# Nine instead of twelve unread matmuls ahead of x of block 0, and w_v in two transfers

## The chip, the cores and the metric

The kernel runs on one core of a Trainium2 chip. The metric is the device time in microseconds of one execution; for the kernel before it is the median of four runs. The engines are named as the profile names them: PE (TensorE, matmul), PEld (its weight load), DVE (VectorE), ACT (ScalarE), POOL (GpSimd) and SP (SyncE). POOL and SP issue nearly all DMA transfers.

## The reference

Two layers follow each other, in fp32, with B = 4, N = 6208 and C = 256. The first is an attention between channels: q and k are divided by their norms over the 6208 rows, their 256 x 256 product goes through a softmax, and v is multiplied by it. The second is a channel mix on x, the first one's output: each row is blended with the row before it, once for k and once for r.

```
qn = q / (norm(q, axis=1) + 1e-6);   kn = k / (norm(k, axis=1) + 1e-6)
a  = softmax(kn.T @ qn / tau, axis=-1)          # per batch 256 x 256
x  = v @ a                                      # B x 6208 x 256
x_prev = x moved down by one row, zeros first
xk = mu_k * x + (1 - mu_k) * x_prev
xr = mu_r * x + (1 - mu_r) * x_prev
k  = max(xk @ w_k, 0)                           # w_k: 256 x 1024
out = sigmoid(xr @ w_r) * (k * k @ w_v)         # w_v: 1024 x 256, w_r: 256 x 256
```

## The kernel before

The rows of a batch go in 12 groups of 512 and one of 64. The program has a head for batch 0 and then one long loop; the instruction order of every engine is fixed by the order in which the program is written (the planner that could reorder it is off).

**The head.** SP loads q and k of batch 0 in fp32 (line 102). DVE casts each piece to bf16, ACT squares it, and PE adds the product of k and q into `s_ps` (line 152) and the squares into `nq_ps` and `nk_ps` (line 119). Once the last k piece is in, the end of the softmax runs as a chain over the engines: POOL takes the root of the norms of k (line 165), DVE their inverse (170, 172), ACT the exponential with row sums (208), DVE the inverse sums and the scaled matrix `a_sb`, in two halves of 128 rows (617, 618). Meanwhile PE transposes v of block 0 (line 258) and one small matmul turns `mu` (604). Then PE runs `filler(F1)` (line 605, the matmuls at line 198): F1 matmuls of 512 columns whose sum nobody reads. After them comes x of block 0, `x_first` (line 279): four matmuls that need both halves of `a_sb`, in the order first half for both column halves, then second half. ACT casts one column half of x to bf16 (281) and DVE the other (282).

**The loop.** A block is 512 rows of one batch; there are 48 of them and one more block for the left-over rows. The work of a block is cut in eight steps `j`, and three blocks are in hand at a time: x and the blends of block i + 2, the up-projection of block i + 1 (`up`, line 343, for block 0 partly line 338), and the gate (`gate_mm`, 364) and down-projection of block i (`down`, 403). The first step of `down` takes the feature tiles 0 to 2 of `kk` and `w_v_sb` for a quarter of the rows, the second step tiles 3 to 7, and so on:

```
for fh in (range(3) if h == 0 else range(3, 8)):
    nc.tensor.matmul(v_ps[:, s % 2], kk[:, fh, s * P:(s + 1) * P], w_v_sb[:, fh, :], ...)
```

Between these matmuls PE works on the covariance of the next batch in units (`unit`, 447), for which q and k arrive in groups (`group_load`, 436). ACT casts x and takes the rectifier of the up-projection (347), DVE squares it (354).

**POOL's queue.** The transfers that cast fp32 to bf16 are issued by POOL, in the order of the program: v of block 0, half of w_k, v of block 1, the other half of w_k, v of block 2, the 64-row group of batch 1 (`more_rows(1)`), and then, after the root of line 165, group 0 (`more_rows(2)`), w_r, w_v, v of block 3, group 1 (`more_rows(3)`), v of block 4, and in the loop the further blocks and groups. These transfers take eight semaphores in turn, so POOL issues each only once the transfer eight places ahead of it has landed; some wait besides for their buffer. The first down-projection matmul of the loop waits for w_v's semaphore; the first gate matmul waits for w_r's.

Of the kernel before, what the change touches and what calls it, by code (L numbers as in the profile page):

```python
# [18 lines left out]
def kernel(  # L19
# [13 lines left out]
    nc = tc.nc  # L33
# [3 lines left out]
    P = 128  # L37
# [37 lines left out]
    w_v_sb = const.tile([P, 8, D], BF16, name="w_v_sb")  # L75
# [15 lines left out]
    hk = {}  # L91
    NF = 8
    LEAD = 8
    F1, FQ, F3 = 12, 3, 0
    NPE = 4

    NW = 2
# [137 lines left out]
    def v_load(i):  # L235
        b, t = blocks[i]
        v_bf = pq.tile([P, S, C], BF16, name="v_bf", tag="b2", bufs=NB + 1)
        nc.gpsimd.dma_start(v_bf, v[b, t * M:(t + 1) * M, :].rearrange("(s p) c -> p s c", p=P))  # L238
        st[i, "v"] = v_bf
# [369 lines left out]
    nc.vector.tensor_scalar(omu, mu_k_t, -1.0, 1.0, op0=OP.mult, op1=OP.add)  # L609
    more_rows(2)  # L610
    nc.gpsimd.dma_start(w_r_sb, moe_w_r.rearrange("(ko ki) d -> ki ko d", ki=P))
    nc.gpsimd.dma_start(w_v_sb, moe_w_v.rearrange("(fo fi) d -> fi fo d", fi=P))
    v_load(3)
    more_rows(3)
    v_load(4)
# [23 lines left out]
    for i in range(-2, NBLK):  # L639
        for j in range(8):  # L640
# [32 lines left out]
            if n < NBLK:  # L673

                d = 4 if n != 1 else 3
# [79 lines left out]
```

## Time and profile before

| what | us |
|---|---|
| median of 4 runs | 507.19 (506.98 to 507.80) |
| the profiled execution, its own time | 507.23 |
| its span | 505.5 |
| PE busy | 490.5 (97%) |
| DVE busy | 446.2 (88%) |
| ACT busy | 429.8 (85%) |
| POOL busy | 106.5 (21%) |
| w_v, 512 KB, from issue to landing | 9.4 |
| w_r, 128 KB, from issue to landing | 7.5 |

The span is what the profiler saw from the first to the last instruction; the time of the execution is a little longer. All points of time below count from the span's start. Busy matmul time is modelled at its end,[...] so starts are more exact than ends. A few matmul records are missing from the trace. In the row of 40 slices one slice is 12.6 us and a digit is a share in tenths. In a timeline a line gives the start, the time taken by the run of equal instructions, the engine, the line, the operation and its operands, and in square brackets how long the engine had been idle and what ended that. In the view of waits a line gives who waited for whom, the total in us, how often, and the longest.

### The profile page before, as it was taken

The numbers are of one execution on the slowest core, as the hardware profiler recorded it, in microseconds if no ns is written. First come the engines' busy times: TensorE is split into PE (matmuls) and PEld (weight loads), VectorE is DVE, ScalarE is ACT, GpSimd is POOL, SyncE is SP. The second block draws the span as 40 slices with busy tenths as digits, with TensorE's granted clock in tenths as the row PEclk, the third lists the DMA queues.
The fourth block names the chain that finished last, engine by engine and source line by source line (L and its number), as shares of the span: only waits on it lengthen the run. The fifth ranks groups of instructions, "written<-read, shape, count | busy, mean of one in ns | idle before, by whom it ended". The sixth has DMA issues, their size and how long they took to land.

```text
span 505.5 us, 9692 instructions
## 1 busy us (share of the span) xinstructions
PE 490.5 (97%) x3643; PEld 339.8 (67%) x3706; DVE 446.2 (88%) x704; ACT 429.8 (85%) x806; POOL 106.5 (21%) x150
## 2 busy tenths in 40 slices
PE   5899999999999999999999999999999999999997
PEld 2575677777666766676667666667666666666675
DVE  3568898999999999999999999999999787887875
ACT  6778999999998998998998899899878777777774
POOL 0057523332521321221341132100031000000000
PEclk9999999999999999999999999999999999999999
DMA  8999999999999999899699999973259743344123
GB/s 333 384 334 190 191 202 207 204 198 192 180 179 197 192 195 157 122 169 167 108 183 216 184 173 157 155 149 85 62 113 185 152 99 96 95 78 92 41 84 105
DMA packets 143271, 83.48 MB, mean 165 GB/s; under 512 B 50740, under 2 KB 140024, under 8 KB 143224
## 3 DMA queue, kind: packets, MB, share of 16 engines
q0 software_dynamic: 66080, 33.01, 51.7%
q1 hardware_dynamic: 77000, 49.79, 42.8%
q8 instruction: 29, 0.48, 0.4%
q14 instruction: 18, 0.15, 0.1%
q10 hardware_dynamic: 144, 0.07, 0.0%
HBM read 78.71 MB, written 25.43 MB: 206 GB/s over the span
## 4 chain that ended last, share of the span: by engine, by line
PE 88%; DMA 7%; DVE 1%; issue 1%; ACT 1%; SPq 1%; POOL 1%; ACTq 0%
PE v_ps L403 33%; PE kT_ps L343 30%; PE g_ps L364 9%; PE xT_ps L269 8%; PE s_ps L447 6%; DMA f<-in_k_dram 3%; DMA f<-in_q_dram 2%; DMA w_v_sb<-in_moe_w_v_dram 2%; PE v_ps L392 1%; SPq L102 1%; PE s_ps L152 1%; POOL qk L436 0%; DVE xk L322 0%; DVE kk L354 0%; PE n_ps L502 0%
## 5 line engine op out<-in xcount | busy, mean ns | idle before, releaser
L347 ACT ACTIVATE kr<-kT_ps 128x512 bf16<-128x512 f32 (+1 forms) x392 | 232.5, 597 | 38.1 <-PE kT_ps L343 29.8
L403 PE MATMUL v_ps<-w_v_sb,kk 128*128 128x256 bf16 x1520 | 228.3, 273 | 1.0 <-DMA w_v_sb<-in_moe_w_v_dram 0.2
L343 PE MATMUL kT_ps<-xk,w_k_sb 128*128 128x512 bf16 (+1 forms) x721 | 217.1, 377 | 0.7
L403 PEld LDWEIGHTS <-kk 128*128 128x128 bf16 x1520 | 148.4, 98 | 57.8 <-DVE kk L354 0.4
L354 DVE TENSOR_TENSOR kk<-kr 128x1024 bf16<-128x1024 bf16 (+1 forms) x196 | 132.9, 679 | 30.6 <-ACT kr L347 29.7
L451 ACT ACTIVATE sq<-qk 128x512 f32<-128x512 bf16 (+1 forms) x147 | 93.4, 635 | 0.0
L343 PEld LDWEIGHTS <-w_k_sb 128*128 128x128 bf16 x780 | 75.2, 98 | 22.0 <-issue 0.9
L364 PE MATMUL g_ps<-w_r_sb,xr 128*128 128x256 bf16 x388 | 73.6, 273 | 1.6
L271 ACT CAST X<-xT_ps 128x512 bf16<-128x512 f32 x94 | 55.6, 592 | 19.4 <-PE xT_ps L269 18.7
L322 DVE SCALAR_TENSOR_TENSOR xr<-delta,mu_t,X 128x512 bf16<-128x512 bf16 x96 | 71.2, 743 | 0.0
L364 PEld LDWEIGHTS <-xr 128*128 128x128 bf16 x388 | 37.9, 98 | 44.6 <-issue 0.7
L322 DVE SCALAR_TENSOR_TENSOR xk<-delta,mu_t,X 128x512 bf16<-128x512 bf16 x96 | 67.8, 744 | 0.0
L416 DVE SCALAR_TENSOR_TENSOR res<-res,v_ps 128x512 f32<-128x512 f32 x95 | 64.4, 678 | 0.0
L436 POOL DMA_DIRECT2D qk<-in_q_dram x39 | 28.7, 735 | 159.4 <-ACT sq L451 138.3
L409 ACT ACTIVATE res<-g_ps 128x512 f32<-128x512 f32 x97 | 57.8, 598 | 0.0
L269 PE MATMUL xT_ps<-vT,a_sb 128*128 128x512 bf16 x188 | 56.1, 379 | 0.1
L447 PE MATMUL s_ps<-qk 128*128 128x256 bf16 (+1 forms) x294 | 56.1, 272 | 0.1
L485 DVE TENSOR_TENSOR acc<-acc,sq 128x1024 f32<-128x1024 f32 x44 | 53.5, 1215 | 0.1
L238 POOL DMA_DIRECT2D v_bf<-in_v_dram x48 | 37.0, 773 | 59.6 <-DMA vT<-v_bf 39.5
L447 PEld LDWEIGHTS <-qk 128*128 128x128 bf16 (+1 forms) x294 | 27.8, 98 | 12.3 <-issue 0.8
L311 DVE TENSOR_TENSOR delta<-X 128x1024 bf16<-128x1024 bf16 x48 | 32.9, 685 | 0.1
L436 POOL DMA_DIRECT2D qk<-in_k_dram x39 | 28.7, 736 | 6.5 <-DMA qk<-in_q_dram 2.1
(86 smaller groups left out, 231.6 us busy)
## 6 DMA issues: line engine op xcount, KB each, us to landing
out_dram<-res SPq DMA_DIRECT2D x47, 512.0 KB, 4.2
v_bf<-in_v_dram POOLq DMA_DIRECT2D x48, 256.0 KB, 9.1
qk<-in_q_dram POOLq DMA_DIRECT2D x36, 256.0 KB, 9.6
qk<-in_k_dram POOLq DMA_DIRECT2D x36, 256.0 KB, 10.9
f<-in_q_dram SPq DMA_DIRECT2D x12, 512.0 KB, 7.4
f<-in_k_dram SPq DMA_DIRECT2D x10, 512.0 KB, 8.8
f<-in_k_dram SPq DMA_DIRECT2D x3, 256.0 KB, 7.8
vT<-v_bf SPq DMA_TRANSPOSE x44, 7.7
```

The source lines that it names most:

```text
L269: nc.tensor.matmul(xT_ps, a_sb[:, b, ih, dh * P:(dh + 1) * P], vT[:, :, ih, :], start=ih == 0, stop=ih == 1)
L322: nc.vector.scalar_tensor_tensor(o[:, dh], st[i, "d"][:, dh], mu[:, dh:dh + 1], X[:, dh, c:c + M], op0=OP.mult, op1=OP.add)
L343: nc.tensor.matmul(kT_ps[:, :m], w_k_sb[:, dh, fh * P:(fh + 1) * P], xk[:, dh, :m], start=dh == 0, stop=dh == 1)
L347: nc.scalar.activation(st[i, "kr", fh // 2][:, fh % 2, :m], kT_ps[:, :m], AF.Relu, scale=RH)
L354: nc.vector.tensor_tensor(st[i, "kk"][:, fh - 1:fh + 1, :m], kr[:, :, :m], kr[:, :, :m], op=OP.mult)
L364: nc.tensor.matmul(g_ps[:, s % 2], xr[:, dh, s * P:(s + 1) * P], w_r_sb[:, dh, :], start=s % 2 == 0 and dh == 0, stop=dh == 1, skip_group_ ...
L403: nc.tensor.matmul(v_ps[:, s % 2], kk[:, fh, s * P:(s + 1) * P], w_v_sb[:, fh, :], start=s % 2 == 0 and fh == 0, stop=fh == 7, skip_group_ ...
L409: nc.scalar.activation(st[i, "res"][:, 2 * u:2 * u + 2], st.pop((i, "g", u)), AF.Tanh, scale=0.5)
L416: nc.vector.scalar_tensor_tensor(r, r, 1.0, st.pop((i, "v", u)), op0=OP.add, op1=OP.mult)
L436: nc.gpsimd.dma_start(qk[:rows, :n, i], src_rows(t, b, g))
L447: nc.tensor.matmul(cov[b][:, ih, :], qk[:rows, s, 1, ih * P:(ih + 1) * P], qk[:rows, s, 0, :], start=g == GORD[0] and s == 0 and ih == 0, ...
L451: nc.scalar.activation(G["sq", s // 2][:rows, s % 2], qk[:rows, s], AF.Square)
```

## The change

F1 becomes 9, so three matmuls of `filler(F1)` fall away. The load of w_v, a single transfer on POOL's queue, becomes two in the same place: feature tiles 0 to 2, and then tiles 3 to 7.

```diff
-    F1, FQ, F3 = 12, 3, 0
+    F1, FQ, F3 = 9, 3, 0
...
     nc.gpsimd.dma_start(w_r_sb, moe_w_r.rearrange("(ko ki) d -> ki ko d", ki=P))
-    nc.gpsimd.dma_start(w_v_sb, moe_w_v.rearrange("(fo fi) d -> fi fo d", fi=P))
+
+    w_v = moe_w_v.rearrange("(fo fi) d -> fi fo d", fi=P)
+    nc.gpsimd.dma_start(w_v_sb[:, :3], w_v[:, :3])
+    nc.gpsimd.dma_start(w_v_sb[:, 3:], w_v[:, 3:])
     v_load(3)
     more_rows(3)
     v_load(4)
```

In the instruction order of PE, six rows fall away (three weight loads and three matmuls); POOL has one row more; nothing else changes its place. The first down-projection matmul then waits for the first of the two transfers, and the fourth for the second. From v of block 3 on, every POOL transfer stands one place further in the turn of the eight semaphores.

## The prediction

> **What bounds the kernel now.** I read the page's head first, then the chain that ended last in order of time, then the timelines of PE, DVE, ACT and POOL between 38 and 64 us, and last the transfers' times to landing.
>
> ```profile
> span 505.5 us, 9692 instructions
> PE 490.5 (97%) x3643; PEld 339.8 (67%) x3706; DVE 446.2 (88%) x704; ACT 429.8 (85%) x806; POOL 106.5 (21%) x150
> DMA  8999999999999999899699999973259743344123
> PE f_ps L198 <- DVE qb L134: 6.5, 4, 5.3
> PE s_ps L152 <- DVE kb L147: 1.5, 4, 0.5
> PE v_ps L403 <- DMA w_v_sb<-in_moe_w_v_dram: 0.2, 1, 0.2
> ```
>
> The last three lines are all that the view of waits has for PE over the whole span. The first two belong to the load-bound head before 35 us. The third is the only later one, and it is at the transfer that the change splits. From start to start, PE's matmuls after 57 us follow each other at 0.11 us (256 columns) and 0.22 us (512), apart from holes of one matmul's size, which are lost records. So a microsecond that PE gains before 57 us should still be there at the end, provided that data keep arriving.
>
> ```profile
> 38.46 0.72 POOL nrm_r L165
> 39.18 1.51 POOL qk L436 x2
> 40.69 0.67 POOL w_r_sb L611
> 41.36 9.39 DMA w_v_sb<-in_moe_w_v_dram
> 50.75 0.04 issue
> 50.79 0.49 PE v_ps L403 x3
> ```
>
> This is the chain in order of time. Up to 50.79 us it does not run through PE: it runs through POOL's issues and w_v's transfer, and only from there on PE to the end. Removing unread matmuls alone should therefore buy nothing; w_v would still land at 50.75.
>
> ```profile
> 38.89 2.76 PE L198 MATMUL f_ps<-qb,ident 128*128 128x512 bf16 x11
> 41.49 1.03 PE L279 MATMUL x_ps<-vT,a_sb 128*128 128x512 bf16 x4
> 50.22 0.38 PE L364 MATMUL g_ps<-w_r_sb,xr 128*128 128x256 bf16 x2
> 50.79 0.49 PE L403 MATMUL v_ps<-w_v_sb,kk 128*128 128x256 bf16 x3 [0.20 <-DMA w_v_sb<-in_moe_w_v_dram]
> 52.42 0.71 PE L403 MATMUL v_ps<-w_v_sb,kk 128*128 128x256 bf16 x5
> ...
> 40.44 0.42 DVE L618 TENSOR_TENSOR a_sb<-e_sb,sm 128x256 bf16<-128x256 f32 x1
> 40.98 0.42 DVE L618 TENSOR_TENSOR a_sb<-e_sb,sm 128x256 bf16<-128x256 f32 x1
> 42.55 0.69 DVE L282 CAST X<-x_ps 128x512 bf16<-128x512 f32 x1 [0.75 <-PE x_ps L279]
> ```
>
> Here are the two places of the change. The twelve unread matmuls (eleven recorded, twelve weight loads) end exactly where x of block 0 starts, at 41.49; but x's second factor, a_sb, was complete at 40.98 + 0.42 = 41.40. PE, not the softmax, sets x's start, by little. Later the first three down-projection matmuls wait for w_v; the other five feature tiles are wanted only at 52.42.
>
> **Part 1, nine unread matmuls.** One costs (41.49 - 38.89)/12 = 0.217 us. Three fewer: PE is free at 41.49 - 0.65 = 40.84. x's four matmuls go: both column halves with a_sb's first half, then both with its second. The first half is written at 40.44 + 0.42 = 40.86; in this trace a cast of k ended at 29.09 and its matmuls began at 29.15, so I add 0.06: the first pair starts at 40.92 and has issued by 41.35. The second half is there at 41.40, so the third starts at 41.46, not at 41.49 + 2 x 0.217 = 41.92. **Gain 0.46 of the 0.65 removed**; the rest turns into waits for DVE (0.08 and 0.11).
>
> Does the stage behind follow? ACT casts x's first half at 42.33 and DVE the second at 42.55; 0.46 earlier both are still free (ACT's last scaling of w_k ends at 41.50, DVE's at 41.80). From there ACT and DVE work nearly without a pause up to 50 us and pace PE, but everything hangs on x. Transfers don't move, so each must land before its new need: v of block 1 33.88 + 6.8 = 40.7 (needed 41.9), w_k's second half 34.84 + 7.1 = 41.9 (needed about 46.2), v of block 2 44.3 (47.7), the 64-row k group 44.8 (48.2), the first full k group 39.93 + 7.5 = 47.4 (49.0), w_r 40.67 + 7.5 = 48.2 (49.8). None binds, so PE reaches the first down-projection 0.46 earlier.
>
> [...]
>
> **Part 2, w_v in two transfers.** PE's g_ps pair starts at 50.22 and takes 2 x 0.109, so v_ps could have started at 50.44; it started at 50.79. The stall is 0.35 (the view's 0.20 counts from the modelled end). With part 1 alone it becomes 0.81. Now the first three tiles: the queue delivers in order, w_r has landed at 48.2, and w_v's 512 KB take until 50.75, 2.55 us. Three eighths are 0.96: **landing 49.2**, needed at 50.44 - 0.46 = 49.98. The stall is gone, with 0.8 us to spare. The other five eighths land at 50.75 plus what one transfer more costs; they are needed at 52.42 - 0.81 = 51.6. Spare: 0.85 us.
>
> What does one transfer more cost in the queue? Bounds: nothing, if bytes alone count[...]. The rows: w_r's 128 KB land 0.8 after the transfer ahead of them, and 512 KB at 2.55 would give 0.64 for that size; the two 32 KB pieces of the small group land 0.2 apart, against 0.16. So 0.05 to 0.15 in a full queue; I take 0.1, nearest to w_r, and 50.85 is still in time. [...]I take the rows: the DMA share is 9 tenths in every slice of the first third[...].
>
> POOL issues one instruction more, about 0.75 us like its neighbours. The larger effect is its eight semaphores in turn: each transfer waits for the one eight places before, and now one later.
>
> ```profile
> 41.36 0.94 POOL L612 DMA_DIRECT2D w_v_sb<-in_moe_w_v_dram  x1
> 42.49 0.76 POOL L238 DMA_DIRECT2D v_bf<-in_v_dram  x1 [0.19 <-PE x_ps L279]
> 44.66 0.74 POOL L436 DMA_DIRECT2D qk<-in_q_dram  x1 [1.41 <-DMA v_bf<-in_v_dram]
> 51.03 0.74 POOL L436 DMA_DIRECT2D qk<-in_k_dram  x1 [1.63 <-DMA w_v_sb<-in_moe_w_v_dram]
> ```
>
> w_v's second part waits for w_k's second half (landed 41.9), so it goes out at about 42.2. v of block 3 now waits for v of block 2, which put it at 44.66 (its old successor's place): **2.2 us later than 42.49**. Behind it q and k of group 1 slip to about 45.4 and 46.1, v of blocks 4 to 6 to 46.9, 47.6 and 48.4 (or 0.3 behind w_r's landing, which is POOL's step from 50.75 to 51.03; the same), q of group 2 waits for w_v's first part (49.5 against 48.65), and k of group 2 for the second (51.03, plus the 0.1). From then on each waits for the same predecessor as before. Is the queue empty meanwhile? At 45.4 it still holds q and k of group 0, w_r and w_v, with data up to 50.75, so v of block 3 is about 5 us early for its turn: landings stay in place and cost nothing. If that cover were gone, the next user would be k of group 1, landed 54.7 and needed at 56.82 - 0.81 = 56.0; then k of group 2, landed 51.03 + 11.1 = 62.1, needed at 63.76 - 0.81 = 62.95. Spare 1.3 and 0.85 us (0.75 with the 0.1). SP's transposes of v wait for blocks 4 on, whose landings (56.1 and later) stay.
>
> **Sum.** 0.46 + 0.35 = 0.81 us off. The profiled execution took 507.23 with a span of 505.5; the 1.7 us around it stay, so its like is 506.4, with a span of 504.7. Its time is 0.04 over the median 507.19, so the median becomes **506.4** (-0.16%). After 50 us PE is 0.35 more ahead of ACT and DVE than before; the nearest need is the last kk square, done at 51.67 - 0.46 = 51.2 and read at 52.0. I charge nothing for it. About 0.2%, or 1.0 us, is what a measurement of this kernel can tell from no change; the forecast lies just inside.
>
> **The rivals.**
> - *More falls away.* Between 47.6 and 50.1 PE has small ACT-paced waits, 0.16 + 0.06 + 0.10 + 0.10 + 0.10 = 0.5 us. If the earlier start lets ACT run ahead of PE there, they shrink too: up to 1.3 us off, 505.9. For it: ACT idles 0.3 to 0.8 us around x. Against: ACT itself starts from x.
> - *The gain is absorbed.* The first matmul of x also waits for block 0's transposed v, and ACT is nearly full up to 57 us; if ACT or DVE then holds PE, 0.35 is given back, or a late need swallows all: 0.0 to 0.4 us off, 507.0. Against: DVE idles 1.8 us before 55.93.
> - *The second part is late (slower).* One mechanism: the additional transfer costs e in the queue, and w_v's last five tiles land at 50.75 + e. From e = 0.85 PE waits; at e = 0.85 + 0.81 = 1.66 the kernel is no faster, and each further microsecond is lost whole. [...]at 3 us, with the later groups pushed back too, 508.5. Against it stand the rows of 0.05 to 0.15.
> - *The split does nothing,* because the first matmuls wait for the whole tile: the stall of 0.81 eats part 1, 507.2. As built, the first v_ps waits for the first transfer's semaphore and the fourth for the second's, so this has hardly a chance.
>
> **How the numbers follow.** The sum as worked out: 0.64, its own range 506.05 to 506.75 ([...]a stall that differs by 0.2 between executions, small waits by 0.15); a part of 0.20 of it lies beyond 1.0 us. More falls away: 0.17, faster. Absorbed or without effect: 0.08, same. Second part late: 0.11, of which 0.10 is slower by over 0.2%. So faster 0.37, same 0.53, slower 0.10. The range for 8 in 10 runs from 505.7 (most of the first rival) to 507.5[...], leaving a tenth above and somewhat less below.
>
> **What would show it.** Right: x_ps starts near 40.9 and its third matmul near 41.46; the first v_ps at about 50.0 with no wait for w_v; two landings, near 49.2 and 50.85; v of block 3 issued near 44.7 and landed still near 52; no new PE wait after 57 us. Wrong: a wait of v_ps x5 for w_v, a PE wait on qk near 56 or 63 us, a gap of over 0.2 us before x, or a lower granted clock (1.00 now) in the slices from 38 us.

## The result, and the profile after

The changed kernel takes 506.66 us (median of 40 runs, 506.25 to 507.24) against 507.28 us (60 runs, 506.76 to 507.98): ratio 0.9987, 95% interval 0.9983 to 0.9992. That is 0.62 us less (0.41 to 0.86 by the interval): measurable, but within the 0.2% that the forecast set as its bound. The profiled execution took 506.60 us with a span of 504.7.

The page of the changed kernel, head and row of the DMA engines:

```profile
span 504.7 us, 9687 instructions
PE 490.0 (97%) x3640; PEld 339.2 (67%) x3703; DVE 446.2 (88%) x704; ACT 429.7 (85%) x806; POOL 107.2 (21%) x151
DMA  8999999999999999999699999973259763344123
```

All that PE waited for over the span (who waited for whom, us in total, times, longest). The line for w_v is gone and nothing has come in its place; the two that are left belong to the head before 35 us:

```profile
PE f_ps L198 <- DVE qb L134: 5.7, 2, 5.2
PE s_ps L152 <- DVE kb L147: 2.5, 4, 1.5
```

PE's timeline of the changed kernel around the two places of the change, and DVE's below it:

```profile
38.96 2.12 PE L198 MATMUL f_ps<-qb,ident 128*128 128x512 bf16 x8
41.01 1.14 PE L279 MATMUL x_ps<-vT,a_sb 128*128 128x512 bf16 x4
49.84 0.38 PE L364 MATMUL g_ps<-w_r_sb,xr 128*128 128x256 bf16 x2
50.06 0.49 PE L403 MATMUL v_ps<-w_v_sb,kk 128*128 128x256 bf16 x3
51.69 0.71 PE L403 MATMUL v_ps<-w_v_sb,kk 128*128 128x256 bf16 x5
...
38.29 0.16 DVE L163 COPY nrm_a<-nk_ps 128x2 f32<-128x2 f32 x1 [1.25 <-PE nk_ps L119]
40.52 0.42 DVE L621 TENSOR_TENSOR a_sb<-e_sb,sm 128x256 bf16<-128x256 f32 x1
41.06 0.42 DVE L621 TENSOR_TENSOR a_sb<-e_sb,sm 128x256 bf16<-128x256 f32 x1
```

This execution's loads ended 0.08 us later than those of the profile before: DVE's copy of the last norms of k (line 163) starts at 38.29 instead of 38.21. Its line in the profile before:

```profile
38.21 0.16 DVE L163 COPY nrm_a<-nk_ps 128x2 f32<-128x2 f32 x1 [0.91 <-PE nk_ps L119]
```

Counted from that copy, x starts 2.72 us after it instead of 3.28, and the first down-projection 11.77 us after it instead of 12.58. PE's starts show x's third matmul at 41.54, 0.06 after a_sb's second half is complete (41.06 + 0.42), so DVE sets it now; the experiments with fewer unread matmuls bear this out. The three v_ps matmuls follow g_ps at once (49.84 + 2 x 0.11). From there the two traces take equally long to the end of the span: 505.5 - 50.79 = 454.7 us before and 504.7 - 50.06 = 454.6 after.

The chain that ended last agrees: before, it ran into the loop through POOL's issues and w_v's transfer; now it runs through x and on to the first down-projection on PE, but for 1.02 us of ACT, which copies v's transpose (line 262). It works with modelled ends and does not resolve the 0.06 us between a_sb and x. From its list in order of time:

```profile
39.41 1.67 PE f_ps L198 x7
41.08 1.06 PE x_ps L279 x4
42.14 0.46 PE vT_ps L258 x8
42.63 1.02 ACT vT L262
43.69 0.59 PE xT_ps L269 x2
...
50.23 0.33 PE v_ps L403 x3
```

POOL's timeline of the changed kernel:

```profile
41.44 0.78 POOL L614 DMA_DIRECT2D w_v_sb<-in_moe_w_v_dram  x1
43.83 0.89 POOL L615 DMA_DIRECT2D w_v_sb<-in_moe_w_v_dram  x1 [1.62 <-DMA w_k_sb<-in_moe_w_k_dram]
44.82 0.77 POOL L238 DMA_DIRECT2D v_bf<-in_v_dram  x1
50.97 0.75 POOL L436 DMA_DIRECT2D qk<-in_k_dram  x1 [0.88 <-DMA w_v_sb<-in_moe_w_v_dram]
```

w_v's first part landed 7.6 us after its issue, at 49.0, and the second 6.9 us after its own, at 50.7: as a whole no later than the single transfer (50.75). v of block 3 was issued at 44.8 instead of 42.5 and landed at 52.0 instead of 52.1.

### The profile page after: what moved, and what is told of

It is laid out like the page before. It is cut to its first block, busy times and chain, and to the rows that moved or that the text cites. A ratio compares the mean times of both kernels' runs of the same rounds, so it can differ in the third digit from the quotient of the medians.

```text
span 504.7 us, 9687 instructions
## 1 busy us (share of the span) xinstructions
PE 490.0 (97%) x3640; PEld 339.2 (67%) x3703; DVE 446.2 (88%) x704; ACT 429.7 (85%) x806; POOL 107.2 (21%) x151
## 4 chain that ended last, share of the span: by engine, by line
PE 92%; DMA 4%; DVE 1%; ACT 1%; issue 1%; ACTq 0%
PE v_ps L403 33%; PE kT_ps L343 30%; PE g_ps L364 9%; PE xT_ps L269 8%; PE s_ps L447 6%; DMA f<-in_k_dram 3%; PE f_ps L198 2%; DMA f<-in_q_dram 1%; PE v_ps L392 1%; PE s_ps L152 1%; PE vT_ps L258 0%; DVE xk L322 0%; DVE kk L354 0%; PE n_ps L502 0%; ACT kr L347 0%
```

## The experiments

The theory is the sum of the prediction: the two parts stand in series on the way to the first down-projection, so each alone buys little, and the time after that matmul is PE's. A ratio is taken against runs of the kernel before that were made beside the experiment's; their median was 507.42 us for the first experiments and 507.16 for those with three unread matmuls, with the second part later and with four transfers. So ratios compare better than medians. The rivals are that one part carries all, that an additional transfer costs time in the queue, and that the unread matmuls do something for PE's clock.

**Part 1 alone.**

```diff
 (before)
-    F1, FQ, F3 = 12, 3, 0
+    F1, FQ, F3 = 9, 3, 0
```

> Part 1 alone: nine unread matmuls, w_v still in one transfer. My theory (x comes 0.46 us earlier, but w_v's landing near 50.75 sets the first down-projection): no gain, 507.2 to 507.3; x's third matmul near 41.5, and the first v_ps waits 0.7 to 0.9 us and starts between 50.7 and 50.9. Rival (w_v's wait is incidental, the removed matmuls carry the gain): 506.7, like the changed kernel.

Measured: ratio 0.9997 (0.9989 to 1.0004), a median of 507.03 us over 13 runs. No gain that can be told from nothing by this interval. The profile:

```profile
PE v_ps L403 <- DMA w_v_sb<-in_moe_w_v_dram: 0.3, 1, 0.3
...
41.25 9.04 DMA w_v_sb<-in_moe_w_v_dram
...
38.11 0.16 DVE L163 COPY nrm_a<-nk_ps 128x2 f32<-128x2 f32 x1 [1.25 <-PE nk_ps L119]
...
49.66 0.38 PE L364 MATMUL g_ps<-w_r_sb,xr 128*128 128x256 bf16 x2
50.34 0.49 PE L403 MATMUL v_ps<-w_v_sb,kk 128*128 128x256 bf16 x3 [0.29 <-DMA w_v_sb<-in_moe_w_v_dram]
```

x came as early as in the changed kernel (2.71 us after the copy of the norms) and PE then waited for w_v, as forecast; but the stall is 50.34 - 49.88 = 0.46 us and not 0.7 to 0.9, because w_v landed at 50.29 in this execution and not at 50.75. v_ps starts 12.23 us after the copy, just when PE would have been ready with twelve unread matmuls (50.44 - 38.21 before): in this execution the wait took all that part 1 had gained. The miss in size leads to the point on sizes below.

**Part 2 alone.**

```diff
 (changed kernel)
-    F1, FQ, F3 = 9, 3, 0
+    F1, FQ, F3 = 12, 3, 0
```

> Part 2 alone: twelve unread matmuls, w_v in two transfers. My theory: the stall of 0.35 us goes and nothing else, 506.9; the first v_ps starts near 50.4 without a wait. Rival (the split carries the whole gain): 506.7. Rival (the split does nothing by itself): 507.3.

Measured: ratio 0.9997 (0.9989 to 1.0005), median 507.10 us, 13 runs. No wait for w_v is left in the profile:

```profile
38.03 0.16 DVE L163 COPY nrm_a<-nk_ps 128x2 f32<-128x2 f32 x1 [1.23 <-PE nk_ps L119]
...
50.04 0.38 PE L364 MATMUL g_ps<-w_r_sb,xr 128*128 128x256 bf16 x2
50.25 0.49 PE L403 MATMUL v_ps<-w_v_sb,kk 128*128 128x256 bf16 x3
```

v_ps starts right behind g_ps, 12.22 us after the copy of the norms, and ahead of the landing of w_v's second part at 50.6: the first matmuls no longer wait for the whole tile. So twelve unread matmuls without the stall mean 12.22, nine 11.77: the 0.46 us of part 1 show up (0.45) as soon as w_v no longer hides them. Neither part alone measured the changed kernel's ratio. The clearest comparison is with the kernel of six unread matmuls and two transfers below, whose x comes at the same time and whose runs were made beside these: 14 of its 21 lie under 506.82 us, the fastest of the 13 with part 1 alone, and 4 of the 13 with part 2 alone do.

That each part alone buys less than both is shown. That the two gains do not simply add is not shown by the times: a rival in which each part keeps a gain of its own fits both intervals, which reach to 0.56 us less. Against it stands the profile of part 1 alone, in which the gain went into the wait.

**Fewer unread matmuls still.**

```diff
 (changed kernel)
-    F1, FQ, F3 = 9, 3, 0
+    F1, FQ, F3 = 6, 3, 0        # and 3, and 0
```

> Six unread matmuls instead of nine, w_v in two transfers. My theory (a_sb's second half sets x from nine matmuls downwards): the same as the changed kernel, 506.6 to 506.7; x's third matmul still near 41.5, with PE idle for 0.7 us ahead of x. Rival (each matmul taken away brings 0.2 us): 506.0.

> Three unread matmuls, w_v in two transfers: PE idles 1.4 us ahead of x, between the 0.7 us with six (granted clock at least 0.999 in all 21 runs) and the 2.1 us with none (clock 0.995 to 0.997 in 9 of 14 runs, and those 1.2 us longer). My theory now[...]: some runs show 0.995 to 0.997, fewer than with none, at 507.8, the others 506.6. Rival (a fixed length between 1.4 and 2.1 us decides): no run shows it and the median is 506.6 to 506.7.

> No unread matmuls at this place, w_v in two transfers. My theory: the same as the changed kernel, 506.6 to 506.7, with PE idle for about 2.0 us ahead of x and the granted clock unchanged. Rival (the unread matmuls keep PE's clock up[...]):[...] a granted clock under 1.0 from 39 to 45 us.

| unread matmuls | PE idle ahead of x, us | first v_ps after the copy of the norms, us | median us, runs | ratio, 95% interval | mean granted clock of the runs |
|---|---|---|---|---|---|
| 9 (the changed kernel) | 0.09 | 11.77 | 506.66, 40 | 0.9987 (0.9983 to 0.9992) | 0.999 to 1.000 |
| 6 | 0.74 | 11.77 | 506.69, 21 | 0.9986 (0.9980 to 0.9992) | 0.999 to 1.000 |
| 3 | 1.39 | 11.78 | 506.99, 13 | 0.9995 (0.9987 to 1.0004) | 0.999 to 1.000 |
| 0 | 2.14 | 11.78 | 507.68, 14 | 1.0001 (0.9993 to 1.0009) | 0.999 to 1.000 in 5, 0.995 to 0.997 in 9 |

The idle time is counted from the last start of a matmul plus its 0.11 or 0.22 us. With nine or fewer, DVE sets x, and in profiles at full clock the distance to v_ps doesn't move: the theory holds. With six the profile names the wait:

```profile
PE x_ps L279 <- DVE a_sb L621: 0.6, 1, 0.6
...
38.64 1.47 PE L198 MATMUL f_ps<-qb,ident 128*128 128x512 bf16 x6
40.69 1.14 PE L279 MATMUL x_ps<-vT,a_sb 128*128 128x512 bf16 x4 [0.58 <-DVE a_sb L621]
```

With none, the theory's 506.6 to 506.7 was wrong for most runs. They fall into two groups: five between 506.33 and 507.06 (median 506.70, as the theory has it) with a clock of 0.999 or 1.000, nine between 507.62 and 507.97 with 0.995 to 0.997. The rival was right in kind: a lower clock in nine of 14 runs. The first profile was one of the five. Two more executions were profiled to catch the other group:

> A second profile of the kernel without unread matmuls at this place, to catch the lower clock that 9 of its 14 runs show. If the idle 2.1 us ahead of x are the cause: in a profile with a mean clock of 0.995 to 0.997 the granted clock is below 1.00 in one stretch[...], and the span is near 506.0. If the clock falls elsewhere: the rows of 38 to 48 us read 1.00.

> The same look once more: [...]one of these two profiles shows it with a chance of about 0.87.

The first took 508.11 us at a mean clock of 0.997, the second 507.25 us at 1.000. Stretches of the first (length, busy time and count of PE, PEld, DVE, ACT and POOL, then the granted clock, the DMA share and GB/s):

```profile
41.50:42.00 0.50, 0.50 (x6) 0.27 (x5) 0.22 (x2) 0.19 (x1) 0.50 (x1) 1.00 1.47 213
42.00:42.50 0.50, 0.50 (x9) 0.50 (x7) 0.47 (x1) 0.40 (x1) 0.27 (x2) 0.59 1.36 177
42.50:43.00 0.50, 0.50 (x4) 0.22 (x2) 0.40 (x2) 0.33 (x1) 0.50 (x1) 0.50 1.46 183
...
45.00:45.50 0.50, 0.50 (x3) 0.23 (x2) 0.50 (x1) 0.27 (x1) 0.50 (x2) 0.50 1.43 193
45.50:46.00 0.50, 0.50 (x4) 0.26 (x3) 0.50 (x2) 0.32 (x1) 0.50 (x2) 0.99 1.45 194
```

and its PE timeline there, against that of the second:

```profile
40.85 1.14 PE L279 MATMUL x_ps<-vT,a_sb 128*128 128x512 bf16 x4 [1.98 <-DVE a_sb L622]
42.45 1.89 PE L338 MATMUL kT_ps<-X,wf 128*128 128x512 bf16 x4
51.09 0.49 PE L403 MATMUL v_ps<-w_v_sb,kk 128*128 128x256 bf16 x3
```

```profile
41.08 1.14 PE L279 MATMUL x_ps<-vT,a_sb 128*128 128x512 bf16 x4 [1.97 <-DVE a_sb L622]
42.68 1.02 PE L338 MATMUL kT_ps<-X,wf 128*128 128x512 bf16 x4
50.13 0.49 PE L403 MATMUL v_ps<-w_v_sb,kk 128*128 128x256 bf16 x3
```

The clock is half of full speed from 42.1 to 45.5 us, 3.4 us long; it falls 1.2 us after PE's idle 2.1 us have ended. The lost clock is 0.5 x 3.4 = 1.7 us, in keeping with the mean of 0.997 over 506.3 us; from 32 to 42 and from 46 to 52 us every stretch of 2 us has 1.00. v_ps comes 12.96 us after the copy of the norms instead of 11.76: 1.2 us late. In all, the 2.1 us of idleness went with a mean clock of 0.995 to 0.997 in 10 of 16 executions, while with 1.4 us none of 13 was below 0.999. The expectation for three, that some runs would lose the clock, missed.

The second execution had the same 2.1 us of idleness, and its clock is 1.00 in every stretch of 2 us from 32 to 52 us. What decides between the two was not shown.

So unread matmuls at this place have a use, the clock; three, six or nine serve it as well as twelve in these runs (0.999 or 1.000 in all 13, 21 and 40). One of the 13 runs with twelve and two transfers had 0.997 and 507.97 us; it was not profiled, and why its clock was lower, with PE kept busy at this place, is open. The median with three is 0.3 us above that with six although its clock never fell; the intervals overlap, and this is left open.

**The second part of w_v later.** It tests how much room the second part has, and whether a late PE gets anything back.

```diff
 (changed kernel)
-    nc.gpsimd.dma_start(w_v_sb[:, 3:], w_v[:, 3:])
     v_load(3)
+    nc.gpsimd.dma_start(w_v_sb[:, 3:], w_v[:, 3:])      # first kernel
     more_rows(3)
+    nc.gpsimd.dma_start(w_v_sb[:, 3:], w_v[:, 3:])      # second kernel
```

> The changed kernel with w_v's second part issued one transfer later, behind v of block 3. My theory (landings follow the order of issue, 256 KB take 1.3 us, and PE needs the part at 51.7): it lands near 52.0, the first of the five matmuls waits 0.3 to 0.4 us, and the time is 507.0. Rival (there is more slack behind the need, or ACT and DVE set the pace): 506.7, like the changed kernel.

> The changed kernel with w_v's second part issued three transfers later, behind group 1. My theory: it lands near 54.7, PE waits 3.0 us, all of it is lost, and the time is 509.6, 2.3 us over the kernel before. Rival (ACT and DVE catch up in the wait and PE wins part of it back): 508.2 or less.

One transfer later: ratio 0.9994 (0.9987 to 1.0001), median 507.05 us, 21 runs. In its profile the part landed at 51.3 and PE, which wanted it at 51.42, did not wait: the queue was 0.4 us early in this execution (w_r landed 9.4 us after the copy of the norms, 9.8 in the changed kernel's). With the median near the expected 507.0 but the changed kernel's ratio at the edge of the interval, this one decides nothing.

Behind group 1: ratio 1.0061 (1.0049 to 1.0074), median 509.84 us, 5 runs; the part landed at 54.6.

```profile
PE v_ps L403 <- DMA w_v_sb<-in_moe_w_v_dram: 2.9, 1, 2.9
...
49.90 0.49 PE L403 MATMUL v_ps<-w_v_sb,kk 128*128 128x256 bf16 x3
...
51.30 0.38 PE L364 MATMUL g_ps<-w_r_sb,xr 128*128 128x256 bf16 x2
54.59 0.71 PE L403 MATMUL v_ps<-w_v_sb,kk 128*128 128x256 bf16 x5 [2.90 <-DMA w_v_sb<-in_moe_w_v_dram]
```

PE's next start could have been 51.53 and was 54.59: a stall of 3.06 us. Three of the five runs kept a clock of 0.999 or more, at 509.67, 509.77 and 509.84: 3.1 us over the changed kernel's 506.66. All of the stall is lost and none is won back, to within the spread of the changed kernel's runs (506.25 to 507.24), against the rival. The other two had 0.996 and 0.997 and took 510.71 and 511.36; neither run was profiled, and whether the stall lowered their clock is not shown.

**Four transfers.**

```diff
 (changed kernel)
-    nc.gpsimd.dma_start(w_v_sb[:, 3:], w_v[:, 3:])
+    nc.gpsimd.dma_start(w_v_sb[:, 3:5], w_v[:, 3:5])
+    nc.gpsimd.dma_start(w_v_sb[:, 5:7], w_v[:, 5:7])
+    nc.gpsimd.dma_start(w_v_sb[:, 7:8], w_v[:, 7:8])
```

> w_v in four transfers of 3, 2, 2 and 1 feature tiles instead of two. My theory (0.1 us per transfer in a full queue): the last part lands at 50.9 to 51.0, needed near 52.1, so the time stays at 506.7; v of block 3 is issued about 1 to 2 us later still and lands near 52.3. [...]

Measured: ratio 0.9993 (0.9985 to 1.0002), median 506.83 us, 13 runs, no wait of PE for w_v. The parts landed at 49.3, 49.9, 50.6 and 51.0, with w_r at 48.35: 2.7 us for the 512 KB, as in the changed kernel (48.05 to 50.73), against 2.6 in one transfer. So two transfers more than in the changed kernel cost the queue nothing that landings to 0.1 us can show. v of block 3 was issued at 46.1 and landed at 52.4, as expected.

## Why the prediction was right

The forecast was 506.4 us (0.81 us less), range 505.7 to 507.5 (the upper end an estimate that no trace shows), most chance on "within 0.2%": the measured 506.66 lies in the range and on the side forecast. The 0.81 us lie inside the measured 0.41 to 0.86, near its end. In the two profiles, the first v_ps comes earlier by just this much, 12.58 - 11.77 = 0.81 us.

- *Part 1, 0.46 us.* Right in mechanism and size: 12.22 against 11.77 us from the copy of the norms to v_ps, without a stall on either side; x's third matmul sits 0.06 us behind a_sb, the step taken from the cast of k.
- *Part 1 alone buys nothing because w_v lands when it lands.* Right in its profile, where the wait grew by the gain; the ratio of 0.9997 fits, but its interval would also hold a gain of 0.46.
- *Part 2, a stall of 0.35 us.* Right in mechanism, and right for the profile it was read from; as a term of a median it is **probably too large**. The figure is one execution's. Nine profiles, two with w_v whole (the first and the third) and seven with it in two parts in the same place, show when the last of it landed, counted from the copy of the norms (to 0.1 us, as the view gives the time from issue to landing): 12.55 (before), 12.44, 12.14, 12.58, 11.90, 12.20, 12.30, 12.05 and, in the last, 11.61 us. With twelve unread matmuls PE is ready at 12.23. Had PE waited for each of these landings (0.04 us from landing to start), the stalls would be 0.36, 0.25, 0, 0.39, 0, 0.01, 0.11, 0 and 0: on average 0.12. The profile before was near the top of its own spread. With 0.12 the sum is 0.46 + 0.12 = 0.58 us, against the measured 0.62. The same list gives part 1 alone: PE is ready at 11.77, starts on average at 12.25 instead of 12.23 + 0.12 = 12.35, and gains 0.10; part 2 alone gains 0.12. Both measured ratios (0.9997, 0.15 us) fit. They would fit the terms of the prediction as well, 0 for part 1 and 0.35 for part 2, so it is the landings that speak for the smaller stall and not the times. That the landing spreads so is shown; what makes it spread was not tried. Issue and landing of the last profile's second part:

```profile
42.28 0.89 POOL L616 DMA_DIRECT2D w_v_sb<-in_moe_w_v_dram  x1
w_v_sb<-in_moe_w_v_dram POOLq DMA_DIRECT2D x1, 320.0 KB, 7.7
```

- *The second part in time.* Right: landed at 50.7, wanted at 51.69. *0.1 us for the additional transfer:* in keeping with 2.7 us in two transfers against 2.6 in one, which is as fine as the landings go.
- *POOL's turn of eight.* Right in kind: v of block 3 issued 2.3 us later (2.2 forecast), landing in place. One step was wrong: w_v's second part went out at 43.8, not 42.2, because w_k's second half landed at 43.5 in this execution instead of 41.9. v of block 3 landed at 52.0 all the same, against 52.1 before.
- *No later wait.* Right: none in the view of waits, and from v_ps to the end of the span both traces take 454.6 to 454.7 us.
- *Rivals.* "More falls away" did not happen: the small ACT-paced gaps between 47 and 50 us are there unchanged, 0.06 to 0.16 us each. "The gain is absorbed" falls with the 454.6 to 454.7 us behind v_ps; "the split does nothing" falls with the profile of part 2 alone, where v_ps starts at 50.25 and the last of w_v lands at 50.6. "The second part is late" is a real price (3.1 us for a landing at 54.6), but the changed kernel is nowhere near it.

## What to carry to other kernels

Two causes in series on the way to one instruction have to be removed together: each edit measured alone could not be told from nothing, and both together gave 0.62 us. A stall read from a single profile is one draw; where its end is a transfer's landing, compare that landing over several profiles, counted from an event on the same path, before it enters a sum. Before unread matmuls are cut, see how long PE would idle in their place. Here they cost time only down to the point where the data set the start: three fewer than twelve brought the first v_ps forward by 0.45 us, and six, nine or twelve fewer by no more. Below that point they can be what holds the clock: with none left and 2.1 us of idleness 10 of 16 executions ran at a mean clock of 0.995 to 0.997, with three left all 13 at 0.999 or 1.000.

## What the runs showed of the hardware that was not expected

An idle stretch of 2.1 us on PE ahead of x went with a lower clock in 10 of 16 executions. In the one of them that was profiled, the granted clock was 0.50 for 3.4 us, beginning 1.2 us after PE had work again, and v_ps came 1.2 us late. With 1.4 us it happened in none of 13, with 0.7 us in none of 21. The landing of the last of w_v, in the same place of a full queue, spread over 1.0 us (11.6 to 12.6 us after the same event) between executions of nearly the same program. A further transfer in that queue took at most some 0.1 us: the 512 KB of w_v took 2.6 us as one transfer and 2.7 us as two and as four.
